# P times V of two heads in one 130-column matmul, in a fused attention and mixture-of-experts kernel

## The chip, the cores and the metric

One core of a Trainium2 chip runs the whole kernel in one launch. The metric is the device time of one execution in microseconds. Three runs of the kernel before took 632.29, 634.75 and 635.75 us, a median of 634.75.

## What is computed

The reference is attention followed by a mixture of experts. Batch 8, 8 heads, 576 positions, 64 channels per head. Of the heads the first four look back over a window of 32 positions, the last four over 128 positions in steps of 4:

```python
scores = scale * np.matmul(q, k.transpose(0, 1, 3, 2))
scores = np.where(masks[None], scores, -1e9)
attn = np.exp(scores - max); attn /= attn.sum(-1) + 1e-09
x = (attn @ v)  ->  4608 tokens of 512 channels
```

Each token then takes the best of 4 groups and in it the best of 4 experts; its row goes through that expert's two layers (512 to 1024, relu, 1024 to 512) and is weighted by the two softmax values of its choices.

## The kernel before, in words

The host reorders the dilated heads so that every head has the same band of 32 positions. One step of the attention loop (36 steps, `NT`) takes 64 positions of 8 heads of two batch entries. The eight heads stand in four slots `c` of two parities `w`. In q and k the two parities share the 128 partitions (64 channels each).

`scores(n)` (line 276) puts the mask into a PSUM tile with one bf16 matmul and adds q times k with 16 fp32 matmuls, which the trace shows as 32 records. VectorE takes the row maximum and the difference, ScalarE the exponential. `transpose_p(n)` turns P so that the keys lie on the partitions: rows 0 to 63 hold the keys of parity 0 and rows 64 to 127 those of parity 1; ScalarE copies the result to `pt`.

`av(n)` (line 309) multiplies P with V. A query block of 32 rows sees 64 keys, which stand either in the V tile `vt` (queries of the second half, a = 1) or in `vs` (a = 0), a copy of V shifted by 32 rows that GpSimd makes in `shift_v` (lines 128 to 132) with four copies of 32 partitions. For each slot, parity, batch entry and half there is one fp32 matmul of 64 rows, 32 columns of weights and 65 columns of V (the 65th is a constant that gives the row's sum): 32 calls, 64 records in the trace. Parity w uses rows 64w to 64w+63 of all operands and writes to PSUM bank w of the tile `o`. ScalarE reads the sums (`den`), VectorE inverts them and multiplies (`normalise`, line 337) into `x`, which is stored to DRAM and transposed for the router.

The order of the work on TensorE, ScalarE, VectorE and SyncE is the order of the program text; GpSimd's is chosen by a scheduler until the expert stage. Step s of the loop issues scores(s), the transposes of P of step s-1, av(s-2), the exponential of s, normalise(s-2), some pieces of the router, then on SyncE the loads of k (for s+3 to s+5), q (s+4) and v (s+3), the two stores of x (s-3), the transposes of x(s-3), and shift_v(s+2). Tiles come from rings: `NQ` = 6 of q, `NK` = 6 of k, `NV` = 7 of vt, `NVS` = 4 of vs, 5 of x. A tile is written again when its last reader is done.

After every ninth step the router works on 1152 tokens: TensorE's small matmuls (lines 378, 389, 440, 511), many short VectorE instructions, spread over the following steps. From the second pair of batch entries on, weights of the first expert are loaded and split into two fp16 halves beside the attention. After the loop come the last router, the order of the experts, and the experts themselves in fp16 pieces (lines 740 and 799). Their tiles lie where the attention's tiles lay.

Of the kernel before, what the change touches and what calls it, by code (L numbers as in the profile page):

```python
# [8 lines left out]
F32 = mybir.dt.float32  # L9
# [3 lines left out]
AF = mybir.ActivationFunctionType  # L13
ALU = mybir.AluOpType
# [3 lines left out]
P = 128  # L18
# [28 lines left out]
NWST2 = 3  # L47
BUDGET = 1.8
COST = (0.21, 0.3, 0.21, 0.62)
NQ, NK, NV, NVS, NPT = 6, 6, 7, 4, 2  # L50
EARLY_STEPS = {NT - 1: 1, NT: 2, NT + 1: 2, NT + 2: 2}
TAIL = (
    "R0w0wr0rrrrrr1rrrrrrrr"
# [12 lines left out]
def moe_attention_kernel(ctx, tc, q, k, v, cmask, wgate, wpack, out):  # L66
    nc = tc.nc
# [11 lines left out]
    id32 = cp.tile([P, P], F32, name="id32")  # L79
# [16 lines left out]
    att = ExitStack()  # L96
    apool = lambda name, bufs=1, **kw: att.enter_context(tc.tile_pool(name=name, bufs=bufs, **kw))
    psA = apool("psA", 1, space=PSUM)
    vp = apool("vp", NV)
    qp = apool("qp", NQ)  # L100
    kr = apool("kp").tile([P, 2, 2 * NK, 8, 32], F32, name="kr")
    pt = [apool(f"pt{i}").tile([P, 4, P], F32, name=f"pt{i}") for i in range(NPT)]
    qb, vt, vs, st, dd, oo, dn = {}, {}, {}, {}, {}, {}, {}

    def load_q(n):
        if n < NT:
            qb[n] = qp.tile([P, 512], F32, name="qb")
            nc.sync.dma_start(qb[n], q[n])
# [5 lines left out]
    def load_k(n, w, steps=2):  # L114
        if n < NT:
            to = kr[w:P:2, w].rearrange("d (b n) s k -> d b n (s k)", b=2)[:, :, n % NK : n % NK + steps]
            nc.sync.dma_start(to, k[n // 2, w].rearrange("d (b n c) -> d b n c", b=2, n=2)[:, :, n % 2 : n % 2 + steps])

    def load_v(n):
        if n < NT:  # L120
            vt[n] = vp.tile([P, 8, 65], F32, name="vt")
            nc.sync.dma_start(vt[n], v[n])

    def shift_v(n):
        vs[n] = vp.tile([P, 8, 65], F32, name="vs", bufs=NVS)
        for r in range(2):
            odd, even = slice(64 * r, 64 * r + 32), slice(64 * r + 32, 64 * r + 64)
            nc.gpsimd.tensor_scalar(vs[n][even], vt[n][even], 1.0, 1.0, ALU.mult, ALU.mult)  # L128
            if n % NJ == 0:
                nc.gpsimd.memset(vs[n][odd], 0.0)  # L130
            else:
                nc.gpsimd.tensor_scalar(vs[n][odd], vt[n - 1][odd], 1.0, 1.0, ALU.mult, ALU.mult)

    nc.vector.memset(kr[:, :, 0 : NK + 1 : NK], 0.0)
    nc.sync.dma_start(masks[:, 0:2], cm[:, 0:2])
# [85 lines left out]
    ap = apool("ap", 3)  # L221
# [29 lines left out]
    def spend(budget):  # L251
        while budget > 0 and not gate:
            got = run(routes)
            if got is None:
                break
            budget -= COST[got]
            if got == 2:
                gate.append(1)

    def scores(n):  # L260
        J = n % NJ
        s = psS.tile([P, 4, 2, 64], F32, name="s", tag="s")
        m = masks[:, MASK_OF.get(J, 1), :]
        nc.tensor.matmul(
            s.rearrange("p (t u) w k -> p t (u w) k", t=2),
            idb,
            m.rearrange("p (t k) -> p t k", t=2).unsqueeze(2).broadcast_to([P, 2, 4, 64]),
            start=True,
            stop=False,
        )  # L270
        qv = qb.pop(n)
        for c in range(4):
            for bb in range(2):
                for a in range(2):
                    sl, j = bb * 4 + c, bb * 2 + a
                    nc.tensor.matmul(
                        s[32 * j : 32 * j + 32, c].rearrange("p w k -> p (w k)"),
                        qv[:, (sl * 2 + a) * 32 : (sl * 2 + a) * 32 + 32],
                        kr[:, :, keys(n, a), sl],
                        start=False,  # L280
                        stop=(c == 3),
                    )
        s = s.rearrange("p c w k -> p (c w) k")
        d = ap.tile([P, 8, 64], F32, name="d", bufs=2)
        mx = ap.tile([P, 8], F32, name="mx")
        nc.vector.tensor_reduce(mx, s, axis=AX.X, op=ALU.max)
        nc.vector.tensor_tensor(d, s, mx.unsqueeze(2).broadcast_to([P, 8, 64]), ALU.subtract)
        dd[n] = d

    def softexp(n):  # L290
        p = ap.tile([P, 8, 64], F32, name="p", bufs=2)
        nc.scalar.activation(p, dd.pop(n), AF.Exp, scale=SCALE)
        st[n] = p

    def transpose_p(n):
        p = st.pop(n)
        t = psT.tile([P, 4, P], F32, name="t", tag="t")
        for c in range(4):
            nc.tensor.transpose(t[:, c, :], p[:, 2 * c : 2 * c + 2, :].rearrange("p a b -> p (a b)"), id32)
        nc.scalar.copy(pt[n % NPT], t)  # L300

    def av(n):
        o = psA.tile([P, 2, 512], F32, name="o", tag="o")
        for c in range(4):
            for w in range(2):
                for bb in range(2):
                    for a in range(2):
                        j = bb * 2 + a
                        nc.tensor.matmul(
                            o[32 * j : 32 * j + 32, w, c * 65 : c * 65 + 65],  # L310
                            pt[n % NPT][64 * w : 64 * w + 64, c, 32 * j : 32 * j + 32],
                            (vs, vt)[a][n][64 * w : 64 * w + 64, bb * 4 + c, :],
                            start=True,
                            stop=True,
                        )
        oo[n] = o
        den = ap.tile([P, 2, 4], F32, name="den")
        ov = o[:, :, 0:260].rearrange("p k (s c) -> p k s c", c=65)
        nc.scalar.activation(den, ov[:, :, :, 64], AF.Copy, bias=1e-9 / SX)
        dn[n] = den  # L320
# [10 lines left out]
    def normalise(n):  # L331
        o = oo.pop(n)
        ov = o[:, :, 0:260].rearrange("p k (s c) -> p k s c", c=65)
        den = dn.pop(n)
        nc.vector.reciprocal(den, den)
        x = ap.tile([P, 4, 2, 64], F32, name="x", bufs=5)
        nc.vector.tensor_tensor(
            x.rearrange("p s w c -> p w s c"),
            ov[:, :, :, 0:64],
            den.unsqueeze(3).broadcast_to([P, 2, 4, 64]),  # L340
            ALU.mult,
        )
        st[n] = x

    def store(n):
        x = st[n]
        bp, J = n // NJ, n % NJ
        for bb in range(2):
            row = (2 * bp + bb) * S + 64 * J
            nc.sync.dma_start(xd[row : row + 64], x[64 * bb : 64 * bb + 64].rearrange("p s w c -> p (s w c)"))  # L350
# [204 lines left out]
    def settle(i):  # L555
        r, off, n, pairs = EARLY[i]
        select(ente[i], cse[i], top[:, r], off // P, n // P)
        found.append(i)
        yield 0
# [305 lines left out]

    start = []
    shift_v(0)
    shift_v(1)
    man = ExitStack()
    ET = mybir.EngineType  # L870
    man.enter_context(tc.manual_schedule(engines={ET.PE, ET.Activation, ET.DVE, ET.SP}))
    for s in range(NT + 3):
        ripe = bool(gate)
        if s < NT:
            scores(s)
        if 0 <= s - 1 < NT:
            transpose_p(s - 1)
        if 0 <= s - 2 < NT:
            av(s - 2)
        if s < NT:  # L880
            softexp(s)
        if 0 <= s - 2 < NT:
            if ripe:
                gate.clear()
            normalise(s - 2)
        if start:
            n = start.pop()
            routes.append(route(n))
            for i, (_, _, _, pairs) in enumerate(EARLY):
                if pairs == n + 1:  # L890
                    routes.append(settle(i))
        spend(BUDGET)
        load_k(s + 4 - s % 2, s % 2)
        load_q(s + 4)
        load_v(s + 3)
        if 0 <= s - 3 < NT:
            store(s - 3)
            transpose_x(s - 3)
        flush()
        if s + 2 < NT:  # L900
            shift_v(s + 2)
        if 2 <= s <= 8 and s % 2 == 0:
            setup(s // 2 - 1)
        for r in picked:
            if r not in ev:
                expert(r)
        if 0 in ev and not wq:
            wq.append(prefetch())
        if s == NT - 1:
            room = fe.tile([P, 48 * P], F16, name="room")  # L910
            cut = lambda a, c: room[:, a * P : (a + c) * P].rearrange("p (c n) -> p c n", c=c)
            for i in range(2):
                xs, hs_ = (cut(24 * i, 4), cut(24 * i + 4, 4)), (cut(24 * i + 8, 8), cut(24 * i + 16, 8))
                eb.append([early(i, xs, lambda hs_=hs_: hs_)])
        if eb:
            run(eb[0], EARLY_STEPS.get(s, 0))
        run(wq)
        if s >= 3 and (s - 3) % NJ == NJ - 1:
            bp = (s - 3) // NJ
            if bp < NBP - 1:  # L920
                start.append(bp)
        run(eq)
# [257 lines left out]
```

## Time and profile before

| | us | share of the span |
|---|---|---|
| profiled execution | 627.64 | |
| its span | 625.8 | |
| TensorE matmul busy | 575.2 | 92% |
| TensorE weight load busy | 402.6 | 64% |
| VectorE busy | 404.0 | 65% |
| ScalarE busy | 330.8 | 53% |
| GpSimd busy | 250.7 | 40% |

The profile is of one execution, with all its times in microseconds from the span's start. Busy is the time in which an engine has an instruction under way; matmuls overlap each other, and small ones in different parts of the array start a few nanoseconds apart, so a busy TensorE is not one at its peak. The granted clock is given as a share of the full clock. A reason in square brackets behind an instruction says how long its engine sat idle before it and what ended that; "issue" means that nothing which the profile shows was waited for. Weight loads of TensorE have rows of their own (PEld).

### The profile page before, as it was taken

Reading aid. Unit: us, or ns where it says so; the run is one execution under the profiler, and the core shown is the slowest. Engines: PE = TensorE matmul, PEld = TensorE weight load, DVE = VectorE, ACT = ScalarE, POOL = GpSimd, SP = SyncE. Lnnn points to the kernel's source line nnn. Section 1 sums busy time; section 2 is a strip of 40 time slices with the busy share of each in tenths; the row PEclk is TensorE's granted clock in tenths of the full one; section 3 lists DMA queues with packets and bytes.
Section 4 is the critical chain, followed back from the end, with each engine's and each line's share of the span. In section 5 each row is a group of like instructions: output and inputs, shape, how many; then the busy total and the mean of one; then the engine's idle time right before and its main releaser. Section 6 shows DMA issues by size and latency. Waiting matters only on the chain.

```text
span 625.8 us, 18720 instructions
## 1 busy us (share of the span) xinstructions
PE 575.2 (92%) x7636; PEld 402.6 (64%) x7636; DVE 404.0 (65%) x849; ACT 330.8 (53%) x662; POOL 250.7 (40%) x304
## 2 busy tenths in 40 slices
PE   5798889988777899989999999999999999999995
PEld 3565767665565677756566666657667667667873
DVE  6764875896976682556576787655556567566820
ACT  2455565486563642655355455545656565656521
POOL 4885554544604271335142443515334233313411
PEclk9999988988989999989999999999999999999999
DMA  7989668499275025667566756767577678678300
GB/s 244 317 252 294 200 211 260 152 336 362 67 218 172 27 76 188 222 229 248 151 196 229 219 167 213 219 186 249 197 226 234 204 233 261 228 245 263 100 29 28
DMA packets 47915, 127.53 MB, mean 204 GB/s; under 512 B 7224, under 2 KB 8126, under 8 KB 47826
## 3 DMA queue, kind: packets, MB, share of 16 engines
q1 hardware_dynamic: 40466, 105.31, 52.8%
q0 software_dynamic: 7360, 20.98, 9.7%
q8 instruction: 62, 1.02, 0.7%
q14 instruction: 27, 0.22, 0.1%
HBM read 107.38 MB, written 19.24 MB: 202 GB/s over the span
## 4 chain that ended last, share of the span: by engine, by line
PE 62%; issue 4%; ACT 2%; DVE 2%; POOL 1%; DMA 1%; POOLq 0%; ACTq 0%
PE y L799 29%; PE a L740 28%; PE pt L721 3%; DMA xr<-xd,sent 1%; POOL out L760 1%; ACT off L247 1%; POOL xr L690 0%; PE tb_ps L511 0%; DVE mv L492 0%; ACT ohl L248 0%; PE lt_ps L378 0%; PE lg_ps L389 0%; POOLq L1063 0%; PE rp L666 0%; DVE room L723 0%
## 5 line engine op out<-in xcount | busy, mean ns | idle before, releaser
L690 POOL DMA_INDIRECT xr<-xd,sent x80 | 98.9, 1237 | 32.6 <-issue 22.6
L799 PEld LDWEIGHTS <-hh 128*128 128x128 f16 (+10 forms) x960 | 68.2, 103 | 58.2 <-issue 3.3
L760 POOL DMA_INDIRECT out<-yr,sent x30 | 30.0, 999 | 180.4 <-ACT yr L773 150.2
L748 DVE SCALAR_TENSOR_TENSOR hl<-a,hh 128x256 f16<-128x256 f32 (+11 forms) x136 | 57.6, 425 | 67.4 <-ACT hh L747 67.3
L747 ACT ACTIVATE hh<-a 128x256 f16<-128x256 f32 (+11 forms) x136 | 52.1, 386 | 53.9 <-PE a L740 53.2
L740 PE MATMUL a<-xh,wb1h 128*128 128x256 f16 (+6 forms) x288 | 77.0, 271 | 0.0
L740 PE MATMUL a<-xl,wb1h 128*128 128x256 f16 (+6 forms) x288 | 76.9, 270 | 0.0
L740 PE MATMUL a<-xh,wb1l 128*128 128x256 f16 (+6 forms) x288 | 76.9, 270 | 0.0
L723 DVE TENSOR_TENSOR xl<-pt,xh 128x512 f16<-128x512 f32 (+10 forms) x42 | 24.9, 595 | 76.5 <-ACT xh L722 76.5
L740 PE MATMUL a<-xh,wa1h 128*128 128x192 f16 (+7 forms) x256 | 71.8, 280 | 0.0
L740 PE MATMUL a<-xl,wa1h 128*128 128x192 f16 (+7 forms) x256 | 71.7, 280 | 0.0
L740 PE MATMUL a<-xh,wa1l 128*128 128x192 f16 (+7 forms) x256 | 71.7, 280 | 0.0
L740 PEld LDWEIGHTS <-wa1h 128*128 128x128 f16 x640 | 59.7, 99 | 14.1 <-issue 2.9
L773 ACT ACTIVATE yr<-y,cs 128x512 f32<-128x512 f32 (+3 forms) x30 | 20.6, 687 | 90.0 <-PE y L799 61.9
L740 PEld LDWEIGHTS <-wb1h 128*128 128x128 f16 x576 | 54.4, 98 | 10.0
L799 PE MATMUL y<-wb2h,hh 128*128 128x512 f16 (+6 forms) x272 | 60.8, 316 | 0.0
L799 PE MATMUL y<-wb2l,hh 128*128 128x512 f16 (+6 forms) x272 | 60.7, 315 | 0.0
L799 PE MATMUL y<-wb2h,hl 128*128 128x512 f16 (+6 forms) x272 | 60.6, 315 | 0.0
L128 POOL TENSOR_SCALAR vs<-vt 32x520 f32<-32x520 f32 x72 | 47.8, 664 | 26.2 <-DMA vt<-v 15.0
L799 PE MATMUL y<-wa2h,hh 128*128 128x512 f16 (+7 forms) x208 | 56.8, 331 | 0.0
L799 PE MATMUL y<-wa2h,hl 128*128 128x512 f16 (+7 forms) x208 | 56.6, 330 | 0.0
L799 PE MATMUL y<-wa2l,hh 128*128 128x512 f16 (+7 forms) x208 | 56.6, 330 | 0.0
(189 smaller groups left out, 1254.4 us busy)
## 6 DMA issues: line engine op xcount, KB each, us to landing
w<-wpack SPq DMA_DIRECT2D x128, 512.0 KB, 4.4
vt<-v SPq DMA_DIRECT2D x36, 260.0 KB, 5.2
qb<-q SPq DMA_DIRECT2D x36, 256.0 KB, 4.6
xd<-x SPq DMA_DIRECT2D x72, 128.0 KB, 4.6
kr<-k SPq DMA_DIRECT2D x34, 256.0 KB, 4.8
xr<-xd,sent POOLq DMA_INDIRECT x80, 4.5
kr<-k SPq DMA_DIRECT2D x4, 128.0 KB, 3.2
out<-yr,sent POOLq DMA_INDIRECT x30, 3.9
```

Of the source, the lines that this page charges most:

```text
L128: nc.gpsimd.tensor_scalar(vs[n][even], vt[n][even], 1.0, 1.0, ALU.mult, ALU.mult)
L247: nc.scalar.activation(off[:, t], low, AF.Square, bias=hi[:, t : t + 1])
L690: nc.gpsimd.indirect_dma_start(out=xr[:, 256 * h : 256 * h + 256], out_offset=None, in_=xd[0:known].rearrange("n (h c) -> (n h) c", h=2), ...
L721: nc.tensor.transpose(pt[:, c, 0:n], xr[0:n, c * P : c * P + P], id32[0:n, 0:n])
L723: nc.vector.tensor_tensor(xl[:, :, t * P : t * P + n], pt[:, :, 0:n], xh[:, :, t * P : t * P + n], ALU.subtract)
L740: nc.tensor.matmul(a[:, 0:cap], ww[:, c * FF + f * P : c * FF + f * P + P], xx[:, c, 0:cap], start=(i == 0), stop=(i == len(mm) - 1),)
L747: nc.scalar.activation(hh[:, f, 0:cap], a[:, 0:cap], AF.Relu)
L748: nc.vector.scalar_tensor_tensor(hl[:, f, 0:cap], a[:, 0:cap], 0.0, hh[:, f, 0:cap], ALU.max, ALU.subtract)
L760: ins = nc.gpsimd.indirect_dma_start(out=out.rearrange("n (g c) -> (n g) c", g=g), out_offset=bass.IndirectOffsetOnAxis(ap=at, axis=0), in ...
L773: nc.scalar.activation(yr[0:n, :], yp[0:n, :], AF.Copy, scale=cs[0:n, t : t + 1])
L799: nc.tensor.matmul(yp[P // g * j : P // g * j + n, 0 : DM // g], h[:, f, t * P : t * P + n], ww[:, f * DM + DM // g * j : f * DM + DM // g ...
```

## The change

V tiles get a second half. A tile is now 128 partitions of two blocks of 520 columns, one block for each parity; rows of parity 0 hold data in block 0 and zero in block 1, rows of parity 1 the other way round. So one matmul of all 128 rows with both blocks as 130 moving columns gives both parities side by side. The zero blocks are written once for each buffer, in steps 0 to 5 (by ScalarE for vt, by VectorE for vs); the buffers are fixed tiles, taken in turn. The v load is two DMAs of 64 partitions. The output tile `o` holds slots 0 and 1 in its first bank and slots 2 and 3 in its second, and the view in `normalise` follows that. The larger tiles are paid for with one buffer less of q, of v and of x. `load_v` before the loop is called for steps 0, 1 and 2, as before.

```diff
-NQ, NK, NV, NVS, NPT = 6, 6, 7, 4, 2
+NQ, NK, NV, NVS, NPT = 5, 6, 6, 4, 2
...
-    vp = apool("vp", NV)
+    vp = [[apool(f"v{k}{i}").tile([P, 2, 520], F32, name=f"v{k}{i}") for i in range(n)] for k, n in enumerate((NV, NVS))]
...
+    HV = (slice(0, 64), slice(64, P))
+
+    def blank(k, n):
+        for w in range(2):
+            t = vp[k][n][HV[w], 1 - w]
+            if k:
+                nc.vector.memset(t, 0.0)
+            else:
+                nc.scalar.activation(t, id32[HV[w], 0:1].broadcast_to([64, 520]), AF.Copy, scale=0.0)
+
     def load_v(n):
         if n < NT:
-            vt[n] = vp.tile([P, 8, 65], F32, name="vt")
-            nc.sync.dma_start(vt[n], v[n])
+            vt[n] = vp[0][n % NV]
+            for w in range(2):
+                nc.sync.dma_start(vt[n][HV[w], w], v[n, HV[w]].rearrange("p s c -> p (s c)"))
 
     def shift_v(n):
-        vs[n] = vp.tile([P, 8, 65], F32, name="vs", bufs=NVS)
-        for r in range(2):
-            odd, even = slice(64 * r, 64 * r + 32), slice(64 * r + 32, 64 * r + 64)
-            nc.gpsimd.tensor_scalar(vs[n][even], vt[n][even], 1.0, 1.0, ALU.mult, ALU.mult)
+        vs[n] = vp[1][n % NVS]
+        for w in range(2):
+            odd, even = slice(64 * w, 64 * w + 32), slice(64 * w + 32, 64 * w + 64)
+            nc.gpsimd.tensor_scalar(vs[n][even, w], vt[n][even, w], 1.0, 1.0, ALU.mult, ALU.mult)
...
     def av(n):
         o = psA.tile([P, 2, 512], F32, name="o", tag="o")
         for c in range(4):
-            for w in range(2):
-                for bb in range(2):
-                    for a in range(2):
-                        j = bb * 2 + a
-                        nc.tensor.matmul(
-                            o[32 * j : 32 * j + 32, w, c * 65 : c * 65 + 65],
-                            pt[n % NPT][64 * w : 64 * w + 64, c, 32 * j : 32 * j + 32],
-                            (vs, vt)[a][n][64 * w : 64 * w + 64, bb * 4 + c, :],
-                            start=True,
-                            stop=True,
-                        )
+            for bb in range(2):
+                for a in range(2):
+                    j = bb * 2 + a
+                    vv = (vs, vt)[a][n].rearrange("p w (s c) -> p w s c", c=65)
+                    nc.tensor.matmul(
+                        o[32 * j : 32 * j + 32, c // 2, c % 2 * 130 : c % 2 * 130 + 130],
+                        pt[n % NPT][:, c, 32 * j : 32 * j + 32],
+                        vv[:, :, bb * 4 + c],
+                        start=True,
+                        stop=True,
+                    )
...
-        x = ap.tile([P, 4, 2, 64], F32, name="x", bufs=5)
+        x = ap.tile([P, 4, 2, 64], F32, name="x", bufs=4)
         nc.vector.tensor_tensor(
-            x.rearrange("p s w c -> p w s c"),
+            x.rearrange("p (k s) w c -> p k (s w) c", k=2),
...
         if s + 2 < NT:
             shift_v(s + 2)
+        if s < NV:
+            blank(0, s)
+        if s < NVS:
+            blank(1, s)
```

## Rows read from the trace of the kernel before

**Rows 1.** The page's chain of waits that ended last, shares of the span by line

```profile
PE y L799 29%; PE a L740 28%; PE pt L721 3%; DMA xr<-xd,sent 1%; POOL out L760 1%; ACT off L247 1%; POOL xr L690 0%; PE tb_ps L511 0%; DVE mv L492 0%; ACT ohl L248 0%; PE lt_ps L378 0%; PE lg_ps L389 0%; POOLq L1063 0%; PE rp L666 0%; DVE room L723 0%
```

**Rows 2.** Busy time by stretch: length, PE, PEld, DVE, ACT, POOL, clock, DMA share, GB/s

```profile
14.00:61.00 47.00, 39.18 (x1185) 27.82 (x1183) 28.63 (x74) 24.19 (x59) 35.85 (x65) 1.00 0.90 292
61.00:118.00 57.00, 51.46 (x1365) 39.35 (x1363) 41.50 (x96) 30.94 (x82) 29.84 (x48) 0.91 0.66 208
118.00:183.00 65.00, 50.62 (x1372) 38.16 (x1369) 55.87 (x130) 41.86 (x105) 29.00 (x39) 0.92 0.74 250
```

**Rows 3.** Tile o's matmuls; then TensorE in one step: start, duration, instruction

```profile
L309 PE MATMUL o<-vs,pt x1152: 213/218/314, 14.1 to 182.0; 64*32 64x65 f32 x192
...
66.29 0.24 PE L309 MATMUL o<-vs,pt 64*32 64x65 f32 x1
...
67.08 0.66 PE L361 MATMUL tx<-id,x 128*128 128x128 f32 x4
...
67.89 1.08 PE L276 MATMUL s<-kr,qb 128*32 128x128 f32 x32
68.90 0.66 PE L299 MATMUL t<-id,p 128*128 128x128 f32 x4
```

**Rows 4.** Waits from 0 to 61 us: who, for whom, total us, times, longest

```profile
PE o L309 <- issue: 4.7, 4, 1.7
```

**Rows 5.** TensorE in time: instructions that ended a stop, with its length

```profile
46.61 0.24 PE L309 MATMUL o<-vs,pt 64*32 64x65 f32 x1 [0.76 <-issue]
...
51.31 0.24 PE L309 MATMUL o<-vt,pt 64*32 64x65 f32 x1 [1.11 <-issue]
...
57.45 0.97 PE L378 MATMUL lt_ps<-xT,wgr 128*32 128x192 f32 x13 [1.53 <-issue]
...
84.47 0.21 PE L309 MATMUL o<-vt,pt 64*32 64x65 f32 x1 [2.64 <-issue]
...
103.93 0.21 PE L309 MATMUL o<-vs,pt 64*32 64x65 f32 x1 [1.03 <-issue]
```

**Rows 6.** The page: busy time with instructions; DMA queues with packets and MB

```profile
PE 575.2 (92%) x7636; PEld 402.6 (64%) x7636; DVE 404.0 (65%) x849; ACT 330.8 (53%) x662; POOL 250.7 (40%) x304
...
q8 instruction: 62, 1.02, 0.7%
```

**Rows 7.** Tile o's instructions in two avs, until the stop: PE and PEld first

```profile
21.60:23.70 2.10, 0.48 (x33) 0.38 (x34) 0.00 (x0) 0.00 (x0) 1.00 0.96 350
26.50:28.40 1.90, 0.78 (x55) 0.63 (x56) 0.00 (x0) 0.00 (x0) 1.00 0.98 336
```

**Rows 8.** TensorE in time: a step at full clock, one after the stop

```profile
61.89 2.19 PE L389 MATMUL lg_ps<-sumsel,lt 128*128 128x20 f32 x18
...
104.17 2.97 PE L389 MATMUL lg_ps<-sumsel,lt 128*128 128x20 f32 x18
...
112.36 0.33 PE L361 MATMUL tx<-id,x 128*128 128x128 f32 x1
```

**Rows 9.** VectorE in time: instructions behind its idle times

```profile
85.52 0.20 DVE L335 RECIPROCAL den<-den 128x8 f32<-128x8 f32 x1 [1.25 <-ACT den L319]
88.59 0.69 DVE L286 TENSOR_REDUCE mx<-s 128x8 f32<-128x512 f32 x1 [1.50 <-PE s L276]
...
151.17 0.69 DVE L286 TENSOR_REDUCE mx<-s 128x8 f32<-128x512 f32 x1 [3.23 <-PE s L276]
```

**Rows 10.** SyncE in time: DMA issues of one step

```profile
46.10 0.88 SPq L117 DMA_DIRECT2D kr<-k  x1
...
47.71 0.38 SPq L122 DMA_DIRECT2D vt<-v  x1
48.18 1.10 SPq L350 DMA_DIRECT2D xd<-x  x2
```

**Rows 11.** The first steps in time: TensorE's scores of step 2, a ScalarE copy

```profile
12.49 1.08 PE L276 MATMUL s<-kr,qb 128*32 128x128 f32 x32 [1.58 <-DMA qb<-q]
...
16.96 0.59 ACT L300 COPY pt<-t 128x512 f32<-128x512 f32 x1 [1.14 <-PE t L299]
```

More of the change, by code (lines that the diff above doesn't have):

```diff
@@ L117, in load_k @@
             nc.sync.dma_start(to, k[n // 2, w].rearrange("d (b n c) -> d b n c", b=2, n=2)[:, :, n % 2 : n % 2 + steps])
+    HV = (slice(0, 64), slice(64, P))
[6 more added lines that the diff above has]
+                nc.scalar.activation(t, id32[HV[w], 0:1].broadcast_to([64, 520]), AF.Copy, scale=0.0)
     def load_v(n):
         if n < NT:
-            vt[n] = vp.tile([P, 8, 65], F32, name="vt")
-            nc.sync.dma_start(vt[n], v[n])
+            vt[n] = vp[0][n % NV]
+            for w in range(2):
+                nc.sync.dma_start(vt[n][HV[w], w], v[n, HV[w]].rearrange("p s c -> p (s c)"))
     def shift_v(n):
-        vs[n] = vp.tile([P, 8, 65], F32, name="vs", bufs=NVS)
-        for r in range(2):
-            odd, even = slice(64 * r, 64 * r + 32), slice(64 * r + 32, 64 * r + 64)
-            nc.gpsimd.tensor_scalar(vs[n][even], vt[n][even], 1.0, 1.0, ALU.mult, ALU.mult)
+        vs[n] = vp[1][n % NVS]
+        for w in range(2):
+            odd, even = slice(64 * w, 64 * w + 32), slice(64 * w + 32, 64 * w + 64)
+            nc.gpsimd.tensor_scalar(vs[n][even, w], vt[n][even, w], 1.0, 1.0, ALU.mult, ALU.mult)
             if n % NJ == 0:
-                nc.gpsimd.memset(vs[n][odd], 0.0)
+                nc.gpsimd.memset(vs[n][odd, w], 0.0)
             else:
-                nc.gpsimd.tensor_scalar(vs[n][odd], vt[n - 1][odd], 1.0, 1.0, ALU.mult, ALU.mult)
+                nc.gpsimd.tensor_scalar(vs[n][odd, w], vt[n - 1][odd, w], 1.0, 1.0, ALU.mult, ALU.mult)
     nc.vector.memset(kr[:, :, 0 : NK + 1 : NK], 0.0)
```

## The prediction

> **What bounds the kernel now.** I read the chain of waits first. It gives 57% of the span to the two matmul lines of the expert layers (y and a) [rows 1], nearly all of it after the last av at 182 us [rows 3]. The change touches nothing there, so the attention's end is what it can move, and the chain carries each microsecond of that to the end.
>
> I then split the attention by stretches [rows 2]. From 14 to 61 us TensorE is busy 39.2 of 47 us with VectorE at 28.6: TensorE sets the pace, with DMA at 0.90 close behind. From 61 to 118 us TensorE has 51.5 of 57 at a granted clock of 0.91. From 118 to 183 us VectorE has 55.9 of 65 and is the bound.
>
> Then TensorE in order of time. One step holds scores, transposes of P, P times V (av), transposes of x. av is 64 records per step and takes 0.79 us from its first start to the start of what follows (66.29 to 67.08) [rows 3]. Scores, 32 records of 128 rows, 32 columns of weights and 128 moving columns, take 1.01 us (67.89 to 68.90) [rows 3].
>
> Not every step runs like that. In eleven places of the attention TensorE stops with "issue" as the reason, inside av most often; up to 61 us these stops add up to 4.7 in av and 1.5 in the route's matmul at 57.45, 6.2 us [rows 4, 5]; later ones are longer, up to 2.64 us [rows 5]. I take them for waits on the engine's own instructions. The queue named "instruction" moved 62 packets of together 1.02 MB, 16.5 KB each [rows 6], and TensorE's 2 x 7636 matmul and weight-load instructions make 246 for each packet, some 125 pairs of load and matmul. A step has 33 + 4 + 64 + 4 = 105 pairs, and of av 33 records stand before the stop of one step and 55 before that of the next, 22 more, where a period of 127 pairs would put them [rows 7]. From one stop's end to the next it took 46.61 to 51.31 = 4.7 us and 51.31 to 57.45 = 6.1 us [rows 5]. So a block of code is used up before the next has come, where av eats 128 instructions in 0.8 us.
>
> The Trainium skill (Runtime: NRT & Kernel Launch, section Instruction fetch mechanics) says that code comes in blocks of 16 KiB, 256 instructions, over the sequencer's own queue while the block before runs, and that this is hidden because dispatch is slower than the fill. The trace agrees on the block's size and not on the hiding. By the page there would be nothing to win and the change would only cost; that is rival 1.
>
> Some of these stops are followed by a lower granted clock (0.91 and 0.92 in the two later stretches [rows 2], a mix of the levels 1.2 and 2.4 GHz). From the logits' matmuls to the x transposes of the next step the trace has 61.89 to 67.08 = 5.2 us in an undisturbed step, and 104.17 to 112.36 = 8.2 us after the stop at 103.93 [rows 3, 5, 8]: 3.0 us more.
>
> **The change part by part.**
>
> *av, fewer and wider records.* 64 records of 64 rows and 65 columns become 32 of 128 rows and 130 columns. The trace has no such record; its twin is the scores' burst. Taken by columns: 1.01 x 130 / 128 = 1.03 us, so +0.24 us a step. From below: no change, if the 64 issues are what takes the 0.79 us; less is excluded, since four column groups stream 8 x 130 columns each where eight streamed 8 x 65. From above: twice as long, +0.79. I take the twin. Where TensorE sets the pace this is paid: 11 steps to 61 us, some 9 between 84 and 118 us, 3 or 4 later: 24 x 0.235 = +5.6 us. In the other 12, VectorE sits between TensorE's bursts and is late anyway [rows 2]; if that cover were gone they would cost 2.8 more.
>
> The Trainium skill (TensorEngine Tiling (Array Packing), section Theoretical Speedup) gives a contraction of at most 64 rows up to twice the rate in two row tiles; giving that up would double av. The rows show less: 64 x 65 columns in 0.79 us against 32 x 128 in 1.01 is 1.3 times the rate. The page's factor is rival 4.
>
> *Code.* A step falls from 105 to 73 pairs, so a block lasts 127 / 73 = 1.74 steps. An undisturbed step takes 66.29 to 68.90 and the transposes' 0.66, 3.3 us [rows 3]; with 0.24 more, 1.74 steps are 6.1 us, above the first distance between stops and equal to the second. Most stops should go. What they free, by the stage's next limit: to 61 us all 6.2. At 84.47 VectorE had been working without a gap until the stop, so only its idle time behind it is to be had, 1.25 + 1.50 = 2.75 [rows 9]. At 103.93 VectorE is idle anyway, so 1.0 and most of the 3.0 of slow clock: 3.8. After 118 us VectorE is the bound; of the stops there only its one long idle stretch comes back, 3.23 [rows 9]. Together 16.0 us. Some will stay where DMA is dense (6.1 against 6.1 us), so I take three quarters: -12.0. Ends: 0 and -16.0.
>
> *V's loads in two halves.* 36 more DMAs on SyncE, bytes unchanged. In the stretch to 61 us SyncE issues nearly without gap: k at 46.10, v at 47.71, the two stores from 48.18 to 49.28, 3.2 us a step [rows 10]. With 0.38 to 0.55 us (a v load; half of a store) more it needs 3.6 to 3.7, TensorE 3.5. So SyncE's lead of three and four steps hides it, or 0.1 to 0.2 us a step, 1 to 2 us in all, come through; I leave that to the quarter taken off above, and the worse case to rival 2. At the start it is not hidden: scores of step 2 waited 1.58 us for q [rows 11], whose issue now has a half load more before it: +0.5 us (0.4 to 1). GpSimd's first copies of V come later by the same half load, beside it.
>
> *Fewer buffers.* With five q tiles a load waits for the scores of the step before; the k load ahead of it on SyncE waits for those or later ones already. With six v tiles the load at step s waits for av(s-3), and the store of x(s-3) behind it waits for the normalising that follows that av. Behind these waits only loads three and four steps ahead are queued. x with four buffers: the tile is read last by the transposes of the step after. Nothing, up to 1 us.
>
> *Blanks.* Twelve copies on ScalarE in steps 0 to 5, at most 0.59 us each by its copy of 128x512 [rows 11], and eight memsets on VectorE, at most 0.69 each by its pass over 128x512 [rows 9]. They stand last in their step; ScalarE then waits for the transposes, 1.1 us there [rows 11], and VectorE for scores. Nothing; at most 1 us if uncovered. Den, normalising and GpSimd's copies keep their sizes.
>
> **Sum.** +5.6 + 0.5 - 12.0 = -5.9 us. The profiled execution took 627.64 us (span 625.8), so 621.7. The three runs shown have a median of 634.75, 7 us above it; taking the same difference from the median gives 628.9, forecast 629.
>
> **Rivals.**
>
> 1. The stops do not go (slower). A block's arrival is set by the data packets ahead of it in the DMA engines and not by how fast code is used; then they move to other lines, scores and transposes. It decides if more than half of the 16.0 us stays and TensorE's +0.24 is paid in all steps: 8.5 + 0.5, less 0 to 3 us won, gives 641 to 644, taken 642. For it: the DMA share of 0.90, and the 6.1 us. Against it: between 61 and 81 us, where route matmuls of few instructions lie between the steps, no such stop is seen. 0.16.
>
> 2. Another limit takes what is won: SyncE's issuing or the DMA share to 61 us, VectorE after 118 us. Then of the 16.0 only the 3.8 around 104 us are won, against half of av's 5.6 and the 0.5: -0.5, 634, the same as before. For it: the stretch to 61 us and SyncE's step [rows 2, 10]. Against it: SyncE waits for TensorE now, not the other way round. 0.20.
>
> 3. All stops go and av's longer bursts are hidden: -16.0 + 0.5 gives 619. For it: a block's 6.1 us with a fetch of 4.7. Against it: TensorE's 51.5 busy of 57 us leave little to hide in [rows 2]. 0.09.
>
> 4. av takes twice as long: 24 x 0.79 = 19.0 + 0.5 against 12.0 gives 642. Against it: the scores' twin. 0.04.
>
> **How the numbers follow.** The forecast has 0.51, its own range 624 to 633. A measurement of this kernel tells 0.5% (3.2 us) from no change. Faster: nearly all of the forecast, rival 3 and a little of 2: 0.61. Same: most of rival 2 and the forecast's edge: 0.21. Slower: rivals 1 and 4: 0.18. The range from 619 to 642 takes in rival 2 and, since the others scatter about their values, half of each.
>
> **What would show it.** av at 32 records and 1.03 us; stops named "issue" on TensorE in the attention down from eleven to three or less, and some 9 packets fewer on the instruction queue (36 x 64 instructions, 246 to a packet); the clock at full through 100 to 110 us; the last av some 6 us earlier than 182. Wrong if av lasts 1.5 us, if the stops appear in the scores instead, or if TensorE's waits name q, k or v loads.

## The result and the profile after

The change makes the kernel slower: 641.81 us (635.77 to 644.53, nine runs) against 633.02 us of the kernel before on the same chip, a ratio of 1.0119 with a 95% interval of 1.008 to 1.0158, some 7.5 us. Forecast were 629 us and 5.9 us less.

In the page of the kernel after, the chain still goes mostly through the two matmul lines of the experts, as in [rows 1], and the instruction queue moved 53 packets for the 62 of [rows 6], as the prediction said:

```profile
PE 583.3 (91%) x6484; PEld 406.8 (63%) x6484; DVE 408.5 (64%) x857; ACT 336.8 (53%) x674; POOL 247.7 (39%) x304
...
q8 instruction: 53, 0.87, 0.6%
...
PE y L810 31%; PE a L751 29%; PE pt L732 3%; PE o L320 0%; PE tb_ps L522 0%; ACT off L258 0%; PE lt_ps L389 0%; PE lg_ps L400 0%; PE rp L677 0%; POOL out L771 0%; ACT ohl L259 0%; DVE mv L503 0%; DVE wa2l L633 0%; PE t L310 0%; PE tx L372 0%
```

The busy time by stretch of the kernel after, in the columns of [rows 2]:

```profile
14.00:61.00 47.00, 42.75 (x866) 30.96 (x867) 30.57 (x78) 28.33 (x67) 31.69 (x58) 0.97 0.87 238
61.00:118.00 57.00, 51.30 (x1019) 38.84 (x1017) 42.65 (x104) 32.58 (x86) 31.84 (x50) 1.00 0.78 233
118.00:183.00 65.00, 47.60 (x836) 35.52 (x840) 50.95 (x112) 36.08 (x89) 30.43 (x43) 0.85 0.77 242
```

VectorE has 50.95 us where it had 55.87 from 118 to 183 us: less work done in the same time, and TensorE's clock at 0.85. To 61 us the queues moved 238 GB/s instead of 292.

One undisturbed step of TensorE in the kernel after, which answers [rows 3]:

```profile
66.69 1.09 PE L320 MATMUL o<-v,pt 128*32 128x130 f32 x32
67.72 0.66 PE L372 MATMUL tx<-id,x 128*128 128x128 f32 x4
...
68.52 1.08 PE L287 MATMUL s<-kr,qb 128*32 128x128 f32 x32
```

The 32 records take 66.69 to 67.72 = 1.03 us. Waits from 14 to 183 us (who, for whom, total, times, longest), first of the kernel before, then of the kernel after. The rows named issue are the stops in av, of which [rows 4, 5] show some:

```profile
PE o L309 <- issue: 11.5, 8, 2.6
...
POOL vs L128 <- DMA vt<-v: 7.5, 5, 6.1
...
DVE x L337 <- DMA xd<-x: 0.5, 1, 0.5
```

```profile
PE o L320 <- issue: 0.6, 1, 0.6
...
POOL v L139 <- DMA v<-v: 33.5, 17, 7.4
PE s L287 <- DMA kr<-k: 6.7, 9, 1.4
PE s L287 <- DMA qb<-q: 3.3, 1, 3.3
DVE x L348 <- DMA xd<-x: 7.9, 7, 2.3
ACT wa1h L636 <- DMA w<-wpack: 7.3, 1, 7.3
```

So the stops for code went, and waits for transfers came: in the kernel before this view has no row in which TensorE's score matmuls or ScalarE's `wa1h` wait for a load, GpSimd's copies of V (POOL) waited 7.5 us for V, not 33.5, and VectorE's x 0.5 us for a store, not 7.9. The wait of 7.3 us is ScalarE's for an expert's weights. TensorE stands behind it, and its clock falls, as one row in time and one stretch of the kernel after show:

```profile
135.17 1.11 PE L310 MATMUL t<-id,p 128*128 128x128 f32 x4 [6.91 <-ACT p L303]
```

```profile
127.00:136.00 9.00, 1.91 (x36) 1.53 (x36) 1.41 (x4) 3.01 (x9) 3.10 (x5) 0.66 0.88 301
```

All these transfers are SyncE's. Its issues in time (start, length) in the kernel after, against [rows 10]:

```profile
64.70 0.59 SPq L117 DMA_DIRECT2D kr<-k  x1
65.34 0.59 SPq L108 DMA_DIRECT2D qb<-q  x1
66.03 1.13 SPq L133 DMA_DIRECT2D v<-v  x2
67.25 1.20 SPq L361 DMA_DIRECT2D xd<-x  x2
68.50 0.60 SPq L117 DMA_DIRECT2D kr<-k  x1
```

A step is 64.70 to 68.50 = 3.80 us with nothing idle between the issues, and TensorE's step beside it is 3.42 us (av at 66.69, the next at 70.11). V's two halves take 1.13 us where one load took 0.38 to 0.39. Added up over the single issues, SyncE was busy 50.5 of the 57 us from 61 to 118 us, 35.0 in the kernel before (an expectation below has 53.5 for the 50.5). Not every step is that short: the eleven from 64.70 us on take 4.59 us on the mean. Eight issues in the stretch last 1.2 to 2.3 us instead of some 0.6, together 9 us longer; in the kernel before six do, 5 us longer. What holds them up no run shows.

The two profiled spans are 15.0 us apart (640.8 and 625.8). Only 5.1 of that is in the attention: the last av ended at 182.19 before and at 187.31 after. The rest is not the change's (see the end), and single profiles of one kernel differ by 2 to 7 us in this place.

### The profile page after: what moved, and what is told of

Read it like the earlier page. It is cut to its first block, busy times and chain, and to the rows that moved or that the text cites. A ratio compares the mean times of both kernels' runs of the same rounds, so it can differ in the third digit from the quotient of the medians.

```text
span 640.8 us, 16600 instructions
## 1 busy us (share of the span) xinstructions
PE 583.3 (91%) x6484; PEld 406.8 (63%) x6484; DVE 408.5 (64%) x857; ACT 336.8 (53%) x674; POOL 247.7 (39%) x304
## 3 DMA queue, kind: packets, MB, share of 16 engines
q1 hardware_dynamic: 41042, 105.31, 53.5%
## 4 chain that ended last, share of the span: by engine, by line
PE 65%; issue 3%; DVE 1%; ACT 1%; POOL 0%; POOLq 0%; another core or an unknown queue 0%; ACTq 0%
PE y L810 31%; PE a L751 29%; PE pt L732 3%; PE o L320 0%; PE tb_ps L522 0%; ACT off L258 0%; PE lt_ps L389 0%; PE lg_ps L400 0%; PE rp L677 0%; POOL out L771 0%; ACT ohl L259 0%; DVE mv L503 0%; DVE wa2l L633 0%; PE t L310 0%; PE tx L372 0%
## 5 line engine op out<-in xcount | busy, mean ns | idle before, releaser
L701 POOL DMA_INDIRECT xr<-xd,sent x80 | 95.2, 1190 | 34.3 <-issue 21.3
L758 ACT ACTIVATE hh<-a 128x256 f16<-128x256 f32 (+11 forms) x136 | 51.4, 386 | 67.1 <-PE a L751 53.1
L139 POOL TENSOR_SCALAR v<-v 32x520 f32<-32x520 f32 x72 | 46.3, 643 | 61.0 <-DMA v<-v 40.4
```

Source lines behind the costliest of these rows:

```text
L139: nc.gpsimd.tensor_scalar(vs[n][even, w], vt[n][even, w], 1.0, 1.0, ALU.mult, ALU.mult)
L701: nc.gpsimd.indirect_dma_start(out=xr[:, 256 * h : 256 * h + 256], out_offset=None, in_=xd[0:known].rearrange("n (h c) -> (n h) c", h=2), ...
L758: nc.scalar.activation(hh[:, f, 0:cap], a[:, 0:cap], AF.Relu)
```

## The experiments

Theory S: SyncE's chain of issues is the new bound. It includes a wait that the program sets: each transfer on the queues of SyncE and ScalarE together waits until the one eight before it has landed, so there are eight places; GpSimd's queue has eight of its own. (In the first four expectations S is SyncE's issue time alone; the places came in when after_act_queue had missed.) Rivals: B, fewer buffers; T, the longer av; D, two small transfers are worse for the DMA engines than a large one, whoever issues them. In some expectations L stands for S by the number of transfers and their places, I for S by SyncE's issue time alone, N for a price of any further transfer. All ratios are to the kernel before on the same chip.

**V's load split, nothing else** (before_split_v):

```diff
-            nc.sync.dma_start(vt[n], v[n])
+            for w in range(2):
+                h = slice(64 * w, 64 * w + 64)
+                nc.sync.dma_start(vt[n][h], v[n, h])
```

> The kernel before with one thing more: each V load is two DMAs of 64 partitions. Theory S (SyncE's issuing is the new bound: a second half load costs 0.75 us of SyncE a step, 3.2 -> 3.9 us, and loads come late): slower by 4 to 9 us, TensorE's waits name k or q loads. Theory B (the smaller buffer counts make loads late): same within 1 us. Theory T (the longer av): same within 1 us.

1.0204 (1.0164 to 1.0243), 12.7 us of 622: the split alone costs more than the whole change, and more than the 4 to 9 us expected. Its profile has the same waits:

```profile
PE s L278 <- DMA kr<-k: 3.2, 4, 1.6
...
ACT wa1h L627 <- DMA w<-wpack: 7.4, 1, 7.4
```

What is left of the change is worth 1.0119 - 1.0204, about -5.3 us. Theory T cannot explain this run.

The Trainium skill (DMA: Bandwidth & Descriptors, section Rules for kernel authors) advises against two transfers to the two halves of the partitions and for one over all 128, since both share the same engines. The run agrees with the advice: 1.0204. That rule gives no price, and sharing the engines is not the whole reason here, as the runs with halves on GpSimd's queue below show.

**Fewer buffers, nothing else** (before_small_bufs: 5 of q, 6 of v, 4 of x):

> The kernel before with 5 q, 6 v and 4 x buffers in place of 6, 7 and 5, nothing else. Theory S: same within 1 us, SyncE's order hides it. Theory B: slower by 4 to 8 us, with VectorE waiting for the stores of x. Theory T: same.

0.9992 (0.9961 to 1.0022): theory B falls for the kernel before. The changed kernel with its old buffers wasn't tried, so whether fewer buffers cost something once loads are late stays open.

**The second half from ScalarE's queue** (after_act_queue):

```diff
-                nc.sync.dma_start(vt[n][HV[w], w], ...)
+                (nc.sync, nc.scalar)[w].dma_start(vt[n][HV[w], w], ...)
```

> The changed kernel with the second half of each V load issued from ScalarE's queue. Theory S: SyncE back to 3.3 us a step, the k waits of TensorE gone; ScalarE pays some 0.6 us a step, it has room to 118 us; 6 to 12 us faster than the changed kernel, so 0 to 5 us faster than the kernel before. Theories B and T: like the changed kernel, 1.01 of the kernel before.

1.0115 (1.0077 to 1.0154), no better, though SyncE's issuing fell to 37.8 of 57 us: a miss of S as it stood. Issue time alone is not it. SyncE's own waits in that profile, 14 to 183 us:

```profile
SPq L361 <- DMA v<-v: 18.6, 10, 3.7
SPq L117 <- DMA v<-v: 6.5, 4, 3.6
SPq L108 <- DMA v<-v: 5.1, 5, 1.6
```

Stores and loads of q and k wait for V transfers that they have nothing to do with: I read this as the shared places, now held by a queue that stands in ScalarE's order of work.

**Both stores of a step as one transfer** (after_one_store):

```diff
-            nc.sync.dma_start(xd[row : row + 64], x[64 * bb : 64 * bb + 64]...)
+        to = xd[...].rearrange("(b i) c -> b i c", b=2)[:, 64 * J : 64 * J + 64]
+        nc.sync.dma_start(to, x.rearrange("p s w c -> p (s w c)"))
```

> The changed kernel with the two stores of x of a step as one DMA of 128 partitions; the V load stays in two halves. Theory S: SyncE saves 0.6 us a step, as many DMAs in all as before; 6 to 12 us faster than the changed kernel. Theory B: 1.01 of the kernel before, since the stores still wait for the same buffers. Theory T: 1.01.

1.1382 (1.1337 to 1.1428), a miss that tests nothing of S: with this form of store VectorE waits far longer for its buffers.

```profile
DVE x L348 <- DMA xd<-x: 51.4, 18, 4.6
```

The Trainium skill (DMA: Bandwidth & Descriptors, section Rules for kernel authors) says that the outermost size of a pattern caps the number of DMA engines, and it is 2 in this store. The waits fit that; no view here shows a single DMA engine.

**Five transfers a step again, in two ways, beside a repetition.** after_pair_v loads each half for two steps at once, after_zeros_dram keeps the zeros in memory and loads 520 KB in one transfer:

```diff
-                nc.sync.dma_start(vt[n][HV[w], w], v[n, HV[w]]...)
+                nc.sync.dma_start(vring[HV[w], i : i + 2, w], v[n : n + 2, HV[w]]...)
...
+            nc.sync.dma_start(vt[n], v[n])
```

> The changed kernel once more, beside the three below and on the same chip, with a second profile. All theories: 1.008 to 1.016 of the kernel before (1.012 and its interval from the first comparison). What the second profile tells apart: gaps of TensorE in the expert stage that come back are the change's; those that don't are this run's. The waits of the scores on k's loads in the attention should come back, some ten of about 0.9 us each.

> The changed kernel with each half of V loaded for two steps at once (260 KB a transfer, every second step), so that a step has again five transfers on SyncE and not six; bytes and the place of the blank blocks are unchanged, and every half still goes to 64 partitions. Theory L (the number of transfers costs: each takes SyncE's time and one of the eight places for transfers under way): 0.985 to 0.995, the forecast's gain comes through (-5.9 us of 622 is 0.9905), scores wait for k in total under 4 us. Theory D (transfers into 64 partitions move their bytes worse through the DMA engines, however many there are): 1.005 to 1.015, as the changed kernel. Theory T (the longer P times V): 1.005 to 1.015.

> The changed kernel with the zero blocks already in V's array in memory, so that one transfer of 520 KB into all 128 partitions loads a step's V; the twelve blank copies on ScalarE fall away, 260 KB a step are moved more. Theory L: five transfers a step again, but at a DMA share of 0.87 to 0.90 up to 61 us the 11 x 0.26 MB more cost at 292 GB/s 0.9 us a step, some 10 us to 61 us less what the forecast wins: 0.995 to 1.01. Theory D: the same bytes count against full transfers: 0.995 to 1.01, so it tells nothing between these two; theory T (longer P times V, whatever the loads): 1.01 or more on top of the bytes, 1.02. Of interest is where the waits go: by L to loads by bytes to 61 us only, and none after it.

after_again 1.01 (1.0061 to 1.0139), the change again; but its scores wait for k once, 3.8 us, and not some ten times. after_pair_v 0.9901 (0.9864 to 0.9938), after_zeros_dram 0.9896 (0.9859 to 0.9933): with five transfers both are faster than before, the second with 260 KB more a step. T falls. So does the idea that transfers to 64 partitions are slow as such. I had expected the bytes of after_zeros_dram to cost, and they did not. In after_pair_v, TensorE is busier in each stretch than in either kernel, and its clock is back:

```profile
14.00:61.00 47.00, 44.78 (x906) 32.73 (x902) 33.03 (x83) 30.33 (x73) 33.89 (x63) 1.00 0.96 281
61.00:118.00 57.00, 53.68 (x1106) 40.33 (x1099) 48.27 (x117) 35.40 (x96) 33.24 (x54) 1.00 0.88 258
118.00:183.00 65.00, 53.46 (x923) 40.93 (x923) 53.16 (x124) 42.62 (x107) 28.79 (x36) 0.97 0.79 248
```

**A sixth, small transfer added to the kernel before**, in four forms: into one place on SyncE, and into eight places in turn on three queues:

```diff
+            nc.sync.dma_start(tiny, v[n, 64:P, 0, 0:16])                # before_tiny_dma
...
+            nc.sync.dma_start(tiny[:, n % 8], v[n, 64:P, 0, 0:16])      # ..._ring_sync, or nc.scalar, nc.gpsimd
```

> The kernel before, plus one transfer of 64 partitions of 64 bytes each behind every V load, from V to a tile that nobody reads: one more transfer a step (six, as in the changed kernel), nearly no more bytes, V itself still loaded whole. Theory L: 1.008 to 1.02, 5 to 12 us slower, with scores waiting for k. Theory D: within 0.997 to 1.004, since the bytes move as before.

> The kernel before plus one transfer of 64 x 64 bytes a step from V to a tile that nobody reads, now to eight places in turn, so that it never waits for the one of the step before (in the earlier form it did, 7.5 us in all). It takes SyncE's time and one of the eight places that the program gives to transfers under way on the queues of SyncE and ScalarE. Theory L (places): 1.008 to 1.015. Theory I (SyncE's issue time): the same. If the earlier slowdown came from that wait: under 1.004.

> The same small transfer, issued from ScalarE's queue: it takes one of the same eight places, but none of SyncE's time. Theory L (places for transfers under way): 1.006 to 1.015, as with SyncE. Theory I (SyncE's issue time): 0.997 to 1.004.

> The same small transfer, issued from GpSimd's queue, whose transfers have eight places of their own: it takes neither SyncE's time nor one of SyncE's places. Theories L and I: 0.997 to 1.004. Theory N (any further transfer costs, by its 64 packets in the DMA engines): 1.008 to 1.015.

1.0149 (1.0105 to 1.0194), 1.0021 (0.9986 to 1.0056), 1.0161 (1.0107 to 1.0215) and 1.0068 (1.0032 to 1.0104). The second missed what I expected: a sixth transfer of 4 KB on SyncE costs nothing that can be told, though SyncE then issues for 51.4 of 57 us, as long as in the kernel after; neither the count of transfers nor a full SyncE is the price by itself. The first differs from it only in that SyncE waited for the tile of the step before, 7.5 us in ten waits, and that cost 1.3% more: SyncE has no slack for a wait. The fourth lies between the two ranges, so 4 KB on GpSimd's queue cost something too, unexplained. The third is ScalarE's queue again, with SyncE's issuing at 34.7 of 57 us and these waits:

```profile
SPq L118 <- DMA tiny<-v: 16.6, 7, 3.1
SPq L352 <- DMA tiny<-v: 12.6, 7, 5.4
SPq L109 <- DMA tiny<-v: 6.3, 4, 2.9
SPq L123 <- DMA tiny<-v: 4.7, 4, 2.9
```

The second is late all the same, as its waits from 14 to 183 us show:

```profile
POOL vs L130 <- DMA vt<-v: 38.8, 20, 7.1
...
ACT wa1h L627 <- DMA w<-wpack: 5.3, 1, 5.3
```

But no score waits for a load there, and TensorE's stops named issue come to 5.5 us instead of 13.5. Late loads may so cover stops that would have come anyway; that is argued, no run separates it.

**Code by itself** (before_half_records; since its output goes other ways through the experts, only its attention is compared):

```diff
+            w, c2 = c % 2, c // 2 * 2
...
-                            o[32 * j : 32 * j + 32, w, c * 65 : c * 65 + 65],
+                            o[32 * j : 32 * j + 32, w, c2 * 65 : c2 * 65 + 130],
```

> The kernel before, with P times V in 32 records of 64 rows and 130 columns instead of 64 of 64 and 65: as many columns on each part of the array (0.79 us a step, if columns set it), half the records, 73 pairs of load and matmul a step as in the changed kernel; V's loads, V's tiles and the buffers are those of before. It leaves out half of the products (two of four slots of P meet each half of V). It measures the term Code by itself. Theory C (fewer instructions remove TensorE's stops, worth three quarters of 16.0 us): the stops named issue fall from eleven to at most three, 12 us less, 0.981; with all of it 0.975. Rival (the stops go, but other limits take what is won): 0.995 to 1.0. If P times V is set by its records and lasts 0.4 us instead of 0.79, some 5 us more are won by either.

Its last av ends at 161.47 us, 182.19 in the kernel before and 175.38 in before_again below: 14 to 21 us earlier. TensorE has no wait named issue left in the attention. av itself takes 69.93 to 70.53 = 0.60 us:

```profile
69.93 0.29 PE L309 MATMUL o<-vs,pt 64*32 64x130 f32 x1
...
70.53 0.66 PE L361 MATMUL tx<-id,x 128*128 128x128 f32 x4
```

That is 0.19 less than in [rows 3], at most 4.6 us over 24 steps; the rest, 9 to 16 us, I put down to Code, predicted at 12.0 with 16.0 as its end. The columns on each part of the array are those of before, so the time of the 64 records hangs on their number more than on their columns. Its total of 765.38 us says nothing here.

**The sixth transfer on GpSimd's queue**, with V in halves as in the change, beside before_again (the kernel before, unchanged) and the paired loads once more:

```diff
+                (nc.sync, nc.gpsimd)[w].dma_start(vt[n][HV[w], w], ...)    # after_pool_v
...
+            nc.gpsimd.dma_start(qb[n], q[n])                                # after_pool_q
```

> The kernel before once more, with a second profile from the chip of the next three. Its ratio to itself should hold 1 (0.997 to 1.003). What it tells apart: on the later chips the part after the attention lasts 456 to 460 us in the profiles of all variants and 446 to 447 on the first two; if the kernel before shows some 458 there too, that is the chip's, and the attention alone is to be compared.

> The kernel with V loaded for two steps at once, beside the kernel before and the two below on one chip. 0.987 to 0.994, as before; by its profile against before_again's, the attention ends 8 to 13 us earlier and the part after it takes the same time within 2 us. If the part after takes back a third of what the attention wins, the rest of the prediction (that the chain carries each microsecond of the attention to the end) was wrong too.

> The changed kernel with the second half of V issued from GpSimd's queue: SyncE issues five transfers a step as before the change, and these halves take none of the eight places that SyncE's transfers share; still two transfers of 130 KB for V a step. Theory S (SyncE's chain of issues, with its places): 0.990 to 1.0 (the 0.990 of the paired loads, and up to 0.7% that the small transfer on GpSimd's queue cost). Theory D (two small transfers in place of a large one cost in the DMA engines, whoever issues them): 1.008 to 1.016.

> The changed kernel with q's load (256 KB, one a step) issued from GpSimd's queue: again five transfers a step on SyncE, V in two halves as in the change. Theory S: 0.990 to 1.0; SyncE's time spent in issuing falls from 53.5 of 57 us to some 43 between 61 and 118 us, and the load of the expert's weights no longer keeps ScalarE waiting for 4 to 7 us near 135 us. Theory D: 1.008 to 1.016.

before_again 1.0014 (0.9981 to 1.0048). after_pair_v_again 0.9881 (0.9833 to 0.9929), 616.83 us, the fastest version. Its attention, though, ended only 1.0 us earlier than that of before_again in the two profiles, not the 8 to 13 that I expected (169.59 and 182.19 us in the first pair). The two profiled executions took 619.97 and 621.63 us, 1.7 apart, where the medians are 7.3 apart: single profiles scatter, and only the ratios carry the sum. The part after the attention agrees within 0.5 us (443.8 and 444.3).

after_pool_q 0.9955 (0.992 to 0.9989), in the range of S; SyncE issues for 43.5 of 57 us there, and ScalarE's wait for the weights is 0.8 us, as expected. after_pool_v 1.0028 (0.9997 to 1.0059), between S and D. GpSimd's loads stand in front of constants that it makes for the router, and VectorE waited for one of them; 4.69 us in after_pool_q, and in after_pool_v:

```profile
35.49 0.57 DVE L213 TENSOR_SCALAR high<-high 128x64 f32<-128x64 f32 x1 [10.38 <-POOL high L193]
```

**The same from step 12 on**, when these constants are done (`n > 11` in the choice of the queue):

> after_pool_v, but GpSimd's queue issues the second half of V only from step 12 on, when the constants that GpSimd makes in steps 2 to 8 are done (in after_pool_v VectorE waited 10.4 us for one of them at 25 us). Steps 0 to 11 keep six transfers on SyncE. Theory S: 0.986 to 0.996, between the paired loads (0.988 and 0.990) and what the first twelve steps still pay. Theory D (two small transfers cost in the DMA engines whoever issues them): 1.003 to 1.012, no better than after_pool_v.

> The same with q's load instead of V's second half: from step 12 on from GpSimd's queue. Theory S: 0.986 to 0.996, and not worse than after_pool_q (0.9955) with its 4.7 us of waiting for a constant. Theory D: 1.003 to 1.012.

after_pool_v_late 0.9957 (0.9925 to 0.9988): halves of 130 KB, six transfers, and faster than before; D falls. The 0.6 to 0.8% to the paired loads are left: the first twelve steps, GpSimd's queue or a remnant of D. after_pool_q_late 1.0006 (0.9977 to 1.0036) lies between the two and missed: its profile has one new stop of TensorE before a burst of scores, and shortly before that GpSimd had issued four q loads in one go. That the one makes the other is argued, not shown.

```profile
57.94 1.94 PE L287 MATMUL s<-kr,qb 128*32 128x128 f32 x32 [5.97 <-issue]
```

```profile
46.01 2.41 POOL L108 DMA_DIRECT2D qb<-q  x4
```

Where the start of the attention is left out the groups come apart. From the first av instruction of step 11 to that of step 33, in us, one figure for each profile:

| sixth transfer | kernels and profiles | 22 steps |
|---|---|---|
| none | before, before_again, small_bufs | 110.5, 104.6, 108.2 |
| on SyncE or ScalarE | after, after_again, act_queue | 115.0, 108.1, 112.9 |
| on SyncE or ScalarE, old av | split_v, tiny_dma, ring_scalar, ring_sync | 112.3, 113.6, 116.0, 108.3 |
| none, new av | pair_v twice, zeros_dram | 101.2, 104.1, 102.7 |
| on GpSimd, old av | ring_gpsimd | 108.0 |
| on GpSimd, new av | pool_v, pool_q, both late | 103.5, 102.7, 102.9, 102.9 |
| none, half the records | half_records | 98.6 |

With the new av every profile with the sixth transfer off SyncE's and ScalarE's queues needs 101 to 104 us, and every one with it on them 108 to 115; with the old av the groups overlap. Two waits tell the groups apart with either av, from 14 to 183 us. With the sixth transfer on SyncE's or ScalarE's queue (seven profiles) GpSimd's copies wait 33 to 45 us for V, and ScalarE waits once for the expert's weights, 4.4 to 9.1 us. In the twelve others of the table the first is 2 to 10 us (23.5 with the 520 KB of after_zeros_dram) and the second at most 0.8.

## Why the prediction was wrong

**The step that failed** is *V's loads in two halves*: "So SyncE's lead of three and four steps hides it", costed at 0.5 us at the start and 1 to 2 us more at most, with the worse case left to rival 2. Alone it costs 12.7 us. Two things were mis-sized. The added issue was taken as 0.38 to 0.55 us and is 0.75 (1.13 against 0.38), so a SyncE step without a long issue is 3.80 us and not 3.6 to 3.7, against TensorE's 3.42. And SyncE was looked at by the issue times of one short step alone. How the lead is lost is argued: a lead is a stock, and with hardly anything idle between SyncE's issues it isn't refilled, so that every long issue, every store that waits for x and every wait for a place lets the k, q, v and weight loads behind it slip. That SyncE is full is not enough, as before_tiny_ring_sync shows (51.4 of 57 us, 1.0021). The stretches from 61 us on, which the prediction gave to TensorE and VectorE, are where it shows (50.5 of 57 us, and the wait of 7.3 us near 133 us).

**The start**, taken as 0.5 us: scores of step 2 waited 3.34 us for q where they had waited 1.58 [rows 11], and the first av came at 17.20 us (16.05 in after_again), 14.09 before (15.78 in before_again). The direction was right; the size, 0.3 to 3.1 us, two profiles of each don't settle.

**av** was right: 32 records, 1.03 us, twin of the scores. The reason for excluding less, by columns, was not: half_records passes the columns of before in 0.60 us instead of 0.79. On the path it seems to cost somewhat less than the 24 of 36 steps assumed: from half_records to the runs with five transfers, 0.43 us more av a step took 22 steps from 98.6 to about 102.7, 0.19 us a step; that is an estimate from single profiles, of which the three with five transfers alone differ by 2.9.

**Code** was right in mechanism and, as far as single profiles tell, in size: eleven stops to one (0.60 us at 29.74; none in after_again), nine packets fewer, the clock from 100 to 112 us at 1.00 where it was 0.72, 9 to 16 us won where it stands alone. Rival 1 is out.

**Fewer buffers** and **Blanks**: the first nothing, as said, in the kernel before; the second not tried alone, but after_zeros_dram does without ScalarE's twelve copies and is no faster than after_pair_v with them.

**The sum without the failed step** was close: -5.9 us forecast; after_pair_v gives -6.3 us (0.9901 of 634.4) and -7.4 (0.9881 of 623.7). With 12.7 us for the split that makes 5.3 to 6.4 slower, and 7.5 (5 to 10) were measured. Its parts are known to some us only, so some of that closeness is luck.

**The rivals.** Rival 2 named SyncE's issuing and put the result at no change, because it stopped at taking back what was won. A bound that replaces another can lie behind it: this one is later than the old one. That the measured 641.8 us is the 642 of rivals 1 and 4 is coincidence: the stops did go, and av takes 1.03 us. The prediction's own sign for being wrong, TensorE's waits naming q and k loads, is what came.

**Open**: how the price divides between SyncE's issue time and the eight places. The 4 KB transfer fills the one as much and takes the other fully, and costs nothing that can be told; 130 KB cost 2%. The runs show that the price is paid on SyncE's and ScalarE's queues, not how it is paid there.

## What to carry to other kernels

Before a load is split, add up the issuing queue's whole step, with the stores and waits in it, and compare it with the step of the engine that sets the pace: a queue with hardly any idle time left can run late, however far ahead it loads. Here a split that added 0.75 us a step cost 2%, while a 4 KB transfer that added 0.50 cost nothing that can be told. When instructions are merged, count the records, since their number and the blocks of code behind it may be what the time goes to; and get the layout that the merge needs without more transfers, in bigger ones or by another queue whose order is free there.

## What the runs showed of the hardware that was not expected

The part after the last av takes 440 to 444 us in ten profiles and 453 to 457 in eight others, by chip and whatever the kernel (half_records and one_store left out). The profile of the kernel before shown above is of the first sort (443.6) and that of the kernel after of the second (453.5), so 9.9 of the 15.0 us between their spans belong to the chips. The 7 us between the profiled 627.64 us and the three runs, which the prediction carried over, may be of the same kind. The granted clock in that part is 0.98 in the eight and 0.99 in nine of the ten; by these rounded values that is some 4 us, an estimate, and the rest is open. Two profiles from different chips are to be compared stage by stage.

Eight records of 64 rows and 130 columns in different parts of the array pass in 0.11 to 0.13 us (half_records, groups starting at 69.93, 70.06 and 70.17), little more than eight of 65 columns (0.79 us for 64, 0.10 for eight): twice the columns cost 10 to 30% there.
